# Windowed attention and a softplus layer on one core: later w_in transfers behind a maximum, the table of picks in five pieces, a new written-out sequence

## The chip, the cores and the metric

The kernel runs on one core of a Trainium2 chip. The metric is the device time of one execution in microseconds (us). Five engines work side by side: TensorE (PE in the profile, with PEld for its weight loads), VectorE (DVE), ScalarE (ACT), GpSimd (POOL) and SyncE (SP), which here only issues loads. POOL also issues loads (those that cast from 32 to 16 bit) and stores.

## The reference, cut to what matters

```python
# q, k, v: (8, 8, 576, 64) float32; global_idx: 8 positions; w_in (512, 2048), w_out (2048, 512)
scores = q @ k.T / 8
mask = (abs(pos[:, None] - pos[None, :]) <= 32) | is_global[:, None] | is_global[None, :]
attn = softmax(where(mask, scores, -1e9))
x = (attn @ v).transpose(0, 2, 1, 3).reshape(4608, 512)     # heads side by side
h = x @ w_in
out = (max(h, 0) + log1p(exp(-abs(h)))) @ w_out             # softplus between two products
```

## The kernel before, in words

**Tiling.** Each of the 8 batches has 18 blocks of 32 queries. Four blocks in a row (128 tokens, all 8 heads) are a *pair* of score tiles, one for each half of the heads: 36 pairs in all. Four pairs (512 tokens) are a *stage*, 9 stages. For a pair, PE makes scores `s` (`add_pair`), DVE takes the maximum `m`, ACT the exponential into `st` with its sum `sm`, DVE the reciprocal `rs`, POOL or DVE the product `pn` (`no` in the code), and DVE transposes `pn` into `pt` (`tp` in the code). In the first stage the mask is added on PE, by a matmul `s<-mask,ident`, and each half of the heads has its own maximum (`m`, 128x4).

**From attention to the layer.** `add_values` multiplies `pt` with `v` (kept as `vb`) into `xo`, and copies that to `xT`. The first stage is done in three pieces, of one, two and one pairs, the later ones mostly whole. The global columns enter through `vg`, which a chain of its own makes (`add_global`): scores of the global queries `sg`, maximum `gm` and `gnb`, exponential `pg`, transpose `pgt`, product with v `ov`, reciprocal `grs`. `add_moe` multiplies `xT` with the four tiles of `w_in` (`win` 0 to 3, each landing as two transfers) into `h`, ACT makes `g` by softplus, and PE multiplies `g` with `w_out` (`wout` 0 to 3) into `o`.

**Loads.** The q and k of batch 0 come by six loads on SP (`add_parts`): for each of the two, tokens 0-255, tokens 256-511 and the last 64; I call them q0, q1, q2 and k0, k1, k2 (the last 64 tokens are two transfers of 64 KB, the others one of 512 KB). They are cast to `qb` and `kb`, transposed on PE (`tr`) and copied into `qx` and `kx`; `qg` takes the global queries from the matmuls `pick<-hot`, which run over all of q, and the same over all of k fill the global columns of `kx`, which every score tile reads. The v of batch 0 comes by 8 casting transfers on POOL, w_in by 8 more behind a copy that waits for q1 (`T["held"]`), and w_out by 4 behind a copy that waits for batch 1's k1. Batch 1's q and k are queued on SP behind a tiny read of `win` 2 (`trail<-win`), which waits for its landing, and batch 1's v behind a tiny read of `wout` 0.

**What sets the order.** Every piece of work is a job with a cost. A planner (`_Order.run`) follows a written-out sequence of jobs and engines, `ORDER`, so that each engine's queue has a fixed order. The planner's costs (`SWITCH`, `SLOW`, `FETCH`, `moves`, `late`, `hold`) only place idle-time work: where it reckons that PE would stand still before 34 us, `keep` puts matmuls without use (`warm`) that keep PE's clock up. It reckons with PE's instructions being fetched in blocks:

```python
BLOCK = 256
ASK = 130
NEED = 448
```

that is, the first 448 instructions (a matmul and its weight load are two) are there at the start, and each 256 later ones come by a fetch that is asked for a few hundred instructions ahead. From batch 2 on a table `pick`, made by `make_pick` on DVE, gathers the global rows.

Of the kernel before, what the change touches and what calls it, by code (L numbers as in the profile page):

```python
# [20 lines left out]
class _Order:  # L21
# [16 lines left out]
    SWITCH = 107  # L38
# [72 lines left out]
    BEGIN = 3300  # L111
    PACKETS = {1: 1024, 2: 256, 4: 576, 8: 1152}

    def settle(self, dma):
# [1363 lines left out]
```

## Time and profile before

| what | value |
|---|---|
| three runs, us | 332.49, 333.22, 333.39 (median 333.22) |
| the profiled execution, us | 331.16 |
| its span, us | 329.1 |
| PE busy, us | 319.9, of them `warm` 13.9 |
| DVE, ACT, POOL busy, us | 219.9, 233.8, 196.0 |
| transfers | 42.14 MB, 128 GB/s over the span |

The profiled execution is a single one; its span runs from the first to the last instruction, and its own time is 2.1 us longer. Rows of the timeline give the start, the duration, the engine, the line of the kernel, the operation with output and input, and in brackets how long the engine stood idle before and what ended that. A row of the windows gives, for a stretch of time, each engine's busy time and number of instructions, then PE's granted clock (1.00 is full), the busy share of the transfer engines and what they moved.

### The profile page before, as it was taken

The numbers are of one execution on the slowest core, as the hardware profiler recorded it, in microseconds if no ns is written. First come the engines' busy times: TensorE is split into PE (matmuls) and PEld (weight loads), VectorE is DVE, ScalarE is ACT, GpSimd is POOL, SyncE is SP. The second block draws the span as 40 slices with busy tenths as digits, with TensorE's granted clock in tenths as the row PEclk, the third lists the DMA queues.
The fourth block names the chain that finished last, engine by engine and source line by source line (L and its number), as shares of the span: only waits on it lengthen the run. The fifth ranks groups of instructions, "written<-read, shape, count | busy, mean of one in ns | idle before, by whom it ended". The sixth has DMA issues, their size and how long they took to land.

```text
span 329.1 us, 12101 instructions
## 1 busy us (share of the span) xinstructions
PE 319.9 (97%) x5290; PEld 171.3 (52%) x5290; DVE 219.9 (67%) x386; ACT 233.8 (71%) x459; POOL 196.0 (60%) x175
## 2 busy tenths in 40 slices
PE   8878999999999999999999999999999999999996
PEld 3536876565555444544555445445544454454444
DVE  7796689847997799884995975378776970431000
ACT  5698879676798896488558857995749647914622
POOL 7827828996678567969587496738282927230000
PEclk9997999999999999999999999999999999999999
DMA  7998999999889899999999960370010012001002
GB/s 193 187 205 195 198 189 155 157 166 244 136 152 146 152 226 173 180 228 189 178 179 167 155 162 4 127 145 3 4 66 0 36 66 85 13 32 66 34 32 97
DMA packets 168796, 42.14 MB, mean 128 GB/s; under 512 B 153256, under 2 KB 165800, under 8 KB 168744
## 3 DMA queue, kind: packets, MB, share of 16 engines
q1 hardware_dynamic: 155928, 27.15, 46.8%
q0 software_dynamic: 10944, 11.08, 16.9%
q10 hardware_dynamic: 1872, 3.15, 2.5%
q8 instruction: 41, 0.67, 0.9%
q14 instruction: 11, 0.09, 0.1%
HBM read 36.71 MB, written 9.44 MB: 140 GB/s over the span
## 4 chain that ended last, share of the span: by engine, by line
PE 90%; DVE 2%; SPq 2%; DMA 2%; issue 1%; ACT 1%
PE o L1305 39%; PE h L1294 37%; PE xo L1259 4%; PE s L1085 4%; DMA stage<-in_q_dram 2%; PE ov L1005 2%; SPq L522 1%; PE pick L894 1%; SPq L526 1%; PE sg L976 1%; PE warm L737 1%; DVE qx L728 1%; PE tr L865 1%; DVE m L1100 1%; PE pick L907 1%
## 5 line engine op out<-in xcount | busy, mean ns | idle before, releaser
L1305 PE MATMUL o<-wout,g 128*128 128x512 bf16 (+1 forms) x592 | 138.3, 374 | 0.0
L1294 PE MATMUL h<-xT,win 128*128 128x512 bf16 (+3 forms) x768 | 137.8, 328 | 0.1
L1300 ACT ACTIVATE g<-h 128x512 bf16<-128x512 f32 (+3 forms) x192 | 84.5, 503 | 30.0 <-PE h L1294 27.0
L1140 POOL TENSOR_TENSOR pn<-st,rs 128x1024 bf16<-128x1024 f32 (+1 forms) x38 | 66.7, 1766 | 55.7 <-DVE rs L1134 49.9
L1294 PEld LDWEIGHTS <-win 128*128 128x128 bf16 x768 | 67.5, 99 | 59.6 <-issue 0.8
L1305 PEld LDWEIGHTS <-g 128*128 128x128 bf16 x592 | 55.9, 98 | 60.7 <-ACT g L1300 1.0
L1108 POOL TENSOR_TENSOR st<-st,m 128x1024 f32<-128x1024 f32 x32 | 60.2, 1894 | 27.1 <-DVE m L1102 27.0
L1089 DVE TENSOR_TENSOR st<-s,mask 128x512 f32<-128x512 f32 x64 | 41.1, 677 | 18.6 <-PE s L1085 18.4
L1132 DVE TENSOR_REDUCE sm<-st 128x8 f32<-128x1024 f32 x32 | 38.5, 1203 | 14.8 <-ACT st L1125 14.6
L1102 DVE TENSOR_REDUCE m<-st 128x8 f32<-128x1024 f32 x32 | 37.9, 1209 | 0.3
L728 ACT COPY osb<-o 128x512 f32<-128x512 f32 (+1 forms) x30 | 17.2, 577 | 22.6 <-PE o L1305 20.2
L1125 ACT ACTIVATE st<-st 128x1024 f32<-128x1024 f32 x32 | 32.7, 1052 | 0.3
L1149 DVE STREAM_TRANSPOSE pt<-pn 128x512 int32<-128x512 int32 x36 | 24.5, 690 | 5.2 <-POOL pn L1140 5.1
L728 ACT CAST xT<-xo 128x512 bf16<-128x512 f32 (+3 forms) x28 | 11.7, 467 | 18.8 <-PE xo L1259 18.8
L728 DVE CAST xT<-xo 128x512 bf16<-128x512 f32 (+3 forms) x20 | 11.3, 601 | 17.5 <-PE xo L1259 17.4
L1300 ACT ACT_TABLE_LOAD x15 | 19.2, 1283 | 1.7 <-PE h L1294 1.5
L1125 ACT ACT_TABLE_LOAD x14 | 18.0, 1283 | 0.7 <-ACT osb L728 0.4
L725 POOL TENSOR_SCALAR qb<-stage 128x1152 bf16<-128x1152 f32 (+2 forms) x15 | 16.8, 1126 | 2.2 <-issue 1.1
L1085 PE MATMUL s<-kx,qx 64*32 64x128 bf16 x1152 | 14.5, 220 | 3.6 <-issue 2.8
L1085 PEld LDWEIGHTS <-qx 64*32 64x32 bf16 x1152 | 10.4, 90 | 12.2 <-issue 8.9
L728 POOL CAST vb<-stage 128x1152 bf16<-128x1152 f32 x12 | 13.7, 1146 | 3.3 <-DMA stage<-in_v_dram 3.3
L737 PE MATMUL warm<-vb 128*128 128x512 bf16 x46 | 13.9, 451 | 1.3 <-DVE vb L559 1.3
(127 smaller groups left out, 287.2 us busy)
## 6 DMA issues: line engine op xcount, KB each, us to landing
stage<-in_v_dram SPq DMA_DIRECT2D x56, 144.0 KB, 4.2
stage<-in_q_dram SPq DMA_DIRECT2D x48, 144.0 KB, 3.7
stage<-in_k_dram SPq DMA_DIRECT2D x48, 144.0 KB, 4.0
out_dram<-osb POOLq DMA_DIRECT2D x24, 256.0 KB, 3.2
out_dram<-osb ACTq DMA_DIRECT2D x11, 256.0 KB, 2.0
stage<-in_q_dram SPq DMA_DIRECT2D x4, 512.0 KB, 6.2
stage<-in_k_dram SPq DMA_DIRECT2D x4, 512.0 KB, 6.9
win<-in_moe_w_in_dram POOLq DMA_DIRECT2D x8, 256.0 KB, 7.7
```

The source lines that it names most:

```text
L728: {"ACT": nc.scalar.copy, "DVE": V.tensor_copy, "POOL": nc.gpsimd.tensor_copy}[e](out, in_)
L1085: nc.tensor.matmul(out=PS["s", n, g][quad(a), x, :], lhsT=qx[b % 2][rows(g), a, j * BL:(j + 1) * BL], rhs=kx[b % 2][rows(g), a, e0 * BL:(e ...
L1089: V.tensor_tensor(out=PS["st", n][:, h, :, :], in0=PS["s", n, h][:, :, :], in1=mask[:, h, j0:j0 + PB, :, :].rearrange("p j s i -> p j (s i ...
L1102: V.reduce_max(out=m[:], in_=flat(PS["st", n], h0, h1), axis=AX)
L1108: on(e).tensor_tensor(out=t, in0=t, in1=over(PS["m", n, y][:], SL * BL), op=OP.subtract)
L1125: nc.scalar.activation(out=t, in_=t, func=AF.Exp)
L1132: V.reduce_sum(out=sm[:], in_=flat(PS["st", n], h0, h1), axis=AX)
L1140: on(e).tensor_tensor(out=PS["pn", n][:, :, :, h0:h1].rearrange("p x s h -> p h x s"), in0=PS["st", n][:, h0:h1], in1=PS["rs", n, y][:].re ...
L1149: V.transpose(out=bass.AP(base.tensor, base.offset, ap=[list(base.ap[0]), [2 * STEP, PB // 2], [STEP + BL // 2, 2], [1, SL * BL]]), in_=PS ...
L1294: nc.tensor.matmul(out=h[:, :], lhsT=w_in_t[c // 4][:, kd, c % 4 * P:(c % 4 + 1) * P], rhs=PS["xT", m][:, kd, lo:hi], start=(kd == 0), sto ...
L1300: nc.scalar.activation(out=PS["g", m, c][:, lo:hi], in_=PS[key][:, lo_of(c, hi - lo)], func=AF.Softplus)
L1305: nc.tensor.matmul(out=PS["o", m, ns, a][:, :], lhsT=PS["g", m, kf][:, ns * P:(ns + 1) * P], rhs=w_out_t[kf // 4][:, kf % 4, a:z], start=( ...
```

## The change

Three things are done. First, the second transfer of `win` 1 and all that follow it on POOL get a dependence on a new small copy on POOL, `T["seen"]`, which reads the maximum of pair 1 (its second half of the heads). Second, `make_pick` is cut: the clearing and three small steps stay together, and each of the four comparisons is a job of its own. Third, costs of the planner are changed and `ORDER` is replaced by another sequence.

```diff
-    SWITCH = 107
+    SWITCH = 96
...
-    FETCH = 4000
-    SLOW = ((27000, 8000), (34500, 6200), (55000, 8200), (230000, 6000), (1e9, 4500))
+    FETCH = 5500
+    SLOW = ((27000, 6000), (36500, 6800), (60000, 7000), (118000, 5500), (152000, 6300), (230000, 5500), (1e9, 5000))
+    CAP = 7500
...
-                took_ = max(next(x for until, x in self.SLOW if ask < until), self.backlog(ask + 1200) - ask + 2400)
+                took_ = max(next(x for until, x in self.SLOW if ask < until), min(self.backlog(ask + 3000) - ask, self.CAP) + 2400)
...
-    BEGIN = 3300
+    BEGIN = 2900
...
-    FILL, FILLT, NARROW, NFILL, NFILLT = 0.75, 220, 0, 0.8, 140
+    FILL, FILLT, NARROW, NFILL, NFILLT = 0.75, 220, 0, 0.93, 57
...
-    ORDER = (52, 57, 62, 162, 167, 122, 137, 146, 156, 4, 117, 113, 151, 141, 132, 127, 182, 172, 177, 187, 370, 9, 14, 213,
...
+    def make_picks(r):
+        V.tensor_tensor(out=pick[quad(r)].rearrange("p c e g -> p (c e) g")[:, :, r * NG:(r + 1) * NG],
+                        in0=posK[quad(r)].rearrange("p c e -> p (c e)").unsqueeze(2).to_broadcast([BL, 2 * NC, NG]),
+                        in1=gf[quad(r)].unsqueeze(1).to_broadcast([BL, 2 * NC, NG]), op=OP.is_equal)
+
     def make_pick():
...
-        for r in range(R):
...
+    LATER = (1, 1)
...
-            last = T["w_in", x] = o.add({"POOL": (650, 0)}, lambda e, x=x, y=y: weights_in(x, y), [last or T["held"]],
-                                        rank=-1 if x else 0, hold=2000 if x else 0, moves=1340)
+            last = T["w_in", x] = T["w_in", x, y] = o.add({"POOL": (650, 0)}, lambda e, x=x, y=y: weights_in(x, y), [last or T["held"]],
+                                        rank=-1 if x else 0, moves=1340)
+            if (x, y) == LATER:
+                T["later"] = last
...
+        if not m:
+            T["seen"] = o.add(pool(190), lambda e: nc.gpsimd.tensor_copy(seen[:, 0, :], PS["m", 1, 1][:, 0:1]), [T["mx", 1, 1]], rank=0, uses=[("m", 1, 1)])
+            T["later"]["deps"].append(T["seen"])
```

What the new sequence does to the queues shows at three places. On SP, the first loads of batch 0 stood like this before (`stage_60` receives q, `stage_61` k):

```order
L531 DMA gi<-in_global_idx_dram 128x16
L522 DMA stage_60<-in_q_dram 128x8x128
L522 DMA stage_61<-in_k_dram 128x8x128 x2
L522 DMA stage_60<-in_q_dram 128x8x128
L526 DMA stage_61<-in_k_dram 64x4x64 x2
L526 DMA stage_60<-in_q_dram 64x4x64 x2
L765 DMA trail<-win_126 1x2x1
```

and in the changed kernel like this:

```order
L534 DMA gi<-in_global_idx_dram 128x16
L525 DMA stage_61<-in_k_dram 128x8x128 x2
L529 DMA stage_61<-in_k_dram 64x4x64 x2
L525 DMA stage_60<-in_q_dram 128x8x128
L529 DMA stage_60<-in_q_dram 64x4x64 x2
L525 DMA stage_60<-in_q_dram 128x8x128
L769 DMA trail<-win_126 1x2x1
```

All of k now comes first, and q1, which stood fourth, is last.

On POOL, from v's transfers to the first products `pn`, before (`seen` is the small copies' target, `mask<-mask` is `make_ends`):

```order
L725 TENSOR_SCALAR qb_64<-stage0_60 128x2x4x64
L477 DMA vb0_66<-in_v_dram 32x18x64 x8
L1373 COPY seen_110<-stage0_60 128x1
L1356 DMA win0_124<-in_moe_w_in_dram 64x4x512 x2
L671 COPY mask_78<-mask_78 128x2x256
L1356 DMA win1_125<-in_moe_w_in_dram 64x4x512 x2
L1356 DMA win2_126<-in_moe_w_in_dram 64x4x512 x2
L1356 DMA win3_127<-in_moe_w_in_dram 64x4x512 x2
L1140 TENSOR_TENSOR pn_735<-st_415,rs_680 128x512
L1140 TENSOR_TENSOR pn_763<-st_488,rs_731 128x512
```

and now (`pn_533` is pair 0's; pair 0's two stood on DVE before):

```order
L480 DMA vb0_66<-in_v_dram 32x18x64 x2
L1379 COPY seen_110<-stage0_60 128x1
L1360 DMA win0_124<-in_moe_w_in_dram 64x4x512
L675 COPY mask_78<-mask_78 128x2x256
L1360 DMA win0_124<-in_moe_w_in_dram 64x4x512
L1438 COPY seen_110<-m_444 128x1
L1360 DMA win1_125<-in_moe_w_in_dram 64x4x512 x2
L1360 DMA win2_126<-in_moe_w_in_dram 64x4x512 x2
L1144 TENSOR_TENSOR pn_533<-st_316,rs_522 128x512
L1144 TENSOR_TENSOR pn_533<-st_316,rs_511 128x512
L1360 DMA win3_127<-in_moe_w_in_dram 64x4x512
L1144 TENSOR_TENSOR pn_670<-st_404,rs_661 128x512
```

In POOL's queue the new copy stands ahead of the third transfer already, so that six of the eight wait for it, and pair 0's products follow four of them.

On DVE, around the first maxima, before:

```order
L728 COPY kx_70<-tr 128x4x4x32 x2
L723 TENSOR_SCALAR qb<-stage_60 128x256
L1100 TENSOR_REDUCE m<-s 128x4 x2
L728 CAST qg_72<-pick 64x4x8 x2
L728 COPY qx_68<-tr 128x4x128
L1100 TENSOR_REDUCE m<-s 128x4
L982 TENSOR_REDUCE gm<-sg 128x1 x2
L983 TENSOR_REDUCE gnb<-gm 128x1
```

and now:

```order
L727 TENSOR_SCALAR qb<-stage_60 128x256
L647 TENSOR_SCALAR mask<-eqF 128x2x9x8 x2
L732 COPY kx_70<-tr 128x4x4x32
L679 TENSOR_TENSOR own<-posM,gf 128x9x2x8
L727 TENSOR_SCALAR qb<-stage_60 128x2x4x64
L1104 TENSOR_REDUCE m<-s 128x4 x2
L732 COPY qx_68<-tr 128x4x128
L732 CAST qg_72<-pick 64x4x8 x2
L1104 TENSOR_REDUCE m<-s 128x4
L732 COPY qx_68<-tr 128x4x128
L986 TENSOR_REDUCE gm<-sg 128x1 x2
L987 TENSOR_REDUCE gnb<-gm 128x1
```

A cast of one half of q1 (`128x2x4x64`) now stands right ahead of pair 0's maxima; before, it was the cast of q2 (`128x256`).

More of the change, by code (lines that the diff above doesn't have):

```diff
@@ L142, in settle @@
                 sent.append(self.PACKETS[job["units"]])
-            self.backs.append((t, now))
+            if q:
+                self.backs.append((t, now))
             done[q] += 1
@@ L154 @@
     WARM = 0
-    FILL, FILLT, NARROW, NFILL, NFILLT = 0.75, 220, 0, 0.8, 140
-    COLD, COLDT, LONG = 5400, 427, 0.93
+    FILL, FILLT, NARROW, NFILL, NFILLT = 0.75, 220, 0, 0.93, 57
+    COLD, COLDT = 5400, 427
     STARVE = 900
@@ L172, in keep @@
         if t0 < self.COLD:
-            span = (t1 - t0) * self.LONG
+            span = (t1 - t0) * 0.93
             cold = min(span, self.COLD - t0)
@@ L287, in run @@
                 mine = "POOL" if "POOL" in j["cost"] else "SP"
-                dma.append((mine, t + 1500 if j["cost"][e][0] else t, j["moves"], j))
+                dma.append((mine, t + (1900 if mine == "POOL" else 1500) if j["cost"][e][0] else t, j["moves"], j))
                 j["at"] = t
@@ L599, in make_pick @@
                         scalar1=pi[:, 1:2], scalar2=None, op0=OP.add)
-        for r in range(R):
-            V.tensor_tensor(out=pick[quad(r)].rearrange("p c e g -> p (c e) g")[:, :, r * NG:(r + 1) * NG],
-                            in0=posK[quad(r)].rearrange("p c e -> p (c e)").unsqueeze(2).to_broadcast([BL, 2 * NC, NG]),
-                            in1=gf[quad(r)].unsqueeze(1).to_broadcast([BL, 2 * NC, NG]), op=OP.is_equal)
     def make_band():
@@ L759, with follow @@
     followed = set()
-    def follow(x, t):
+    def follow(x, t, row):
         if x in followed:
@@ L764, in follow @@
         followed.add(x)
-        nc.sync.dma_start(out=trail[x:x + 1, :], in_=t[D:D + 1, t.shape[1] - 1, t.shape[2] - 2:])
+        nc.sync.dma_start(out=trail[x:x + 1, :], in_=t[row:row + 1, t.shape[1] - 1, t.shape[2] - 2:])
     def add_load(b, w, deps):
@@ L775, in add_load @@
                     last = T["half", 0, h] = o.add({"POOL": (1300, 0)}, lambda e, h=h, x=x: load_v(nc.gpsimd, 0, h, range(2 * x, 2 * x + 2)), [last], rank=0,
-                                                   moves=1200, late=200)
+                                                   moves=1080, late=200)
                     T["cast", 0, 2].append(last)
@@ L782, in emit @@
                     if behind:
-                        follow(1, w_out_t[0])
+                        follow(1, w_out_t[0], D)
                     load_v(nc.sync, b, h, range(R))
@@ L795, in emit @@
                 if b:
-                    follow(0, w_in_t[2])
+                    follow(0, w_in_t[2], D)
                 load_part(b, w, t)
             T["part", b, w, t] = o.add({"DMA": (700 if b else 0, 0)}, emit, had(("w_in", 2)) + T["cast", 0, w] if b else [], rank=0,
-                                       moves=(1800 if b else 1900) if t < FULL else 900 if b else 650, units=1 if t < FULL else 2)
+                                       moves=1800 if t < FULL else 900 if b else 650, units=1 if t < FULL else 2, late=0 if t < FULL or b else 700)
     def add_cast(b, w):
@@ L947, in add_prep @@
             ws = (1, 0)
-            job = o.add({"PE": (560, 730)}, lambda e, ws=ws: pck(e, ws), [x for w in ws for x in T["cast", b, w]] + [T["make_pick"]],
+            job = o.add({"PE": (560, 730)}, lambda e, ws=ws: pck(e, ws), [x for w in ws for x in T["cast", b, w]] + T["make_picks"],
                         rank=4, array=32, ins=72, opens=[("pick", key)])
@@ L1042, in add_global @@
             ovs.append(o.add({"PE": (72 * n, 72 * n + 170) if b else (110 * n + 100, 110 * n + 240)}, lambda e, m0=m0, m1=m1: ov(e, m0, m1), [tps[-1], *ovs, *T["cast", b, 2]],
-                             rank=3, array=32, ins=16 * n, opens=[] if ovs else [("ov", ("ov", b, y)) for y in range(two)], uses=[("ov", b, y) for y in range(two)] if ovs else []))
+                             rank=3, array=34, ins=16 * n, opens=[] if ovs else [("ov", ("ov", b, y)) for y in range(two)], uses=[("ov", b, y) for y in range(two)] if ovs else []))
         T["gexp", b], T["tpg", b], T["ov", b] = exps[-1], tps[-1], ovs[-1]
@@ L1275, in add_values @@
             last = o.add({"PE": (t, t + 170)}, lambda e, s0=s0, s1=s1: val(e, s0, s1), ready if last is None else [last] + (had(("gv", 0)) if ahead else []),
-                         rank=1, array=64, urgent=last is None, ins=16 * (s1 - s0) + (8 if ahead and s0 == 0 else 0), opens=opened if last is None else [],
+                         rank=1, array=65, urgent=last is None, ins=16 * (s1 - s0) + (8 if ahead and s0 == 0 else 0), opens=opened if last is None else [],
                          uses=[("pt", m)] + ([("xo", v_, r) for r in range(KD)] if last is not None else []))
@@ L1392 @@
     setup("make_own", lambda e: make_own(e), {"DVE": (230, 310)}, [T["make_first"], T["part", 0, 0, 1]], rank=2, port=True)
-    setup("make_pick", lambda e: make_pick(), {"DVE": (1800, 1890)}, [T["make_own"], T["load", 0, 2]], rank=9, hold=18000)
+    setup("make_pick", lambda e: make_pick(), {"DVE": (620, 700)}, [T["make_own"], T["load", 0, 2]], rank=9, hold=18000, port=True)
+    T["make_picks"] = [setup(("make_picks", r), lambda e, r=r: make_picks(r), {"DVE": (310, 390)}, [T["make_pick"]], rank=9, port=True) for r in range(R)]
     setup("blank", lambda e: blank(nc.gpsimd, 1), pool(900), [T["load", 0, 2]], rank=6, hold=11000)
@@ L1439 @@
                 T["w_out", a] = o.add({"POOL": (800, 0)}, lambda e, a=a: weights_out(a),
-                                      [T["landed"], T.get(("w_out", a - 1))], rank=-1, hold=800 if a else 0, moves=2700)
+                                      [T["landed"], T.get(("w_out", a - 1))], rank=-1, moves=2700, late=1500)
         for x in range(len(VALS)):
```

1 line of the change is left out of this document (added), and 143 rows, old and new, of the table ORDER.

## Prediction

> **What bounds the kernel now.** I read the page first: who is busy, and which chain ended last.
>
> ```profile
> PE 319.9 (97%) x5290; PEld 171.3 (52%) x5290; DVE 219.9 (67%) x386; ACT 233.8 (71%) x459; POOL 196.0 (60%) x175
> PE 90%; DVE 2%; SPq 2%; DMA 2%; issue 1%; ACT 1%
> ```
>
> PE is busy for 319.9 of 329.1 us, so 9.2 us are idle, and 90% of the chain is PE. The useful matmuls are the same in both kernels; only what PE loses can change. So I looked for the losses in PE's timeline.
>
> ```profile
> 22.89 0.41 PE L1085 MATMUL s<-kx,qx 64*32 64x128 bf16 x30
> 26.14 0.23 PE L1085 MATMUL s<-kx,qx 64*32 64x128 bf16 x2 [2.84 <-issue]
> 26.30 0.48 PE L1245 MATMUL xo<-vb 128*128 128x128 bf16 x4
> 27.08 0.37 PE L1259 MATMUL xo<-pt,vg 32*64 32x128 bf16 x8
> 28.20 4.33 PE L1294 MATMUL h<-xT,win 128*128 128x128 bf16 x60
> 32.36 0.81 PE L737 MATMUL warm<-vb 128*128 128x512 bf16 x3
> 33.25 0.93 PE L1259 MATMUL xo<-pt,vb 32*64 32x32 bf16 x80
> 34.34 0.39 PE L865 MATMUL tr<-ident,kb 128*128 128x128 bf16 x4
> 45.65 0.38 PE L1305 MATMUL o<-wout,g 128*128 128x512 bf16 x1
> ```
>
> The first layer matmul starts at 28.20. Just before, PE stops after 30 of the 32 matmuls of a score tile and waits 2.84 us for no other engine ("issue"). By the order of the program the two that are late begin at instruction 704, which is 448 + 256: a boundary of the blocks that the code itself names. I read the gap as a late instruction fetch. After 34.34 I found no gap on PE above 0.4 us up to the last matmul, so the game is decided before 45 us. The granted clock shows a second price of the gap:
>
> ```profile
> 25.00:26.00 1.00, 0.00 (x0) 0.00 (x0) 0.50 (x4) 1.00 (x8) 0.48 (x1) 1.00 1.09 182
> 29.00:30.00 1.00, 1.00 (x13) 1.00 (x11) 0.45 (x2) 1.00 (x8) 0.56 (x1) 0.55 1.15 338
> 30.00:31.00 1.00, 1.00 (x22) 1.00 (x20) 0.97 (x3) 0.98 (x7) 0.53 (x1) 1.00 1.19 303
> ```
>
> The clock is 0.55 near 29.5 and full a microsecond later; PE begins 13 matmuls in the one and 22 in the other. At 22 in a microsecond the 60 first `h` need 2.7 us, not 4.33, so the cold clock took 1.6. The Trainium skill (TensorE: Matmul & The Clock Gate, Part 1) has the clock halved after an idle window of about 3.4 us; here 2.84 us of idle were enough, so the row decides, and short gaps may cost clock as well.
>
> **The change, part by part.** First the loads, since q1 is now last of six: two half-microsecond windows, then the page's transfers, and the timelines of POOL and DVE.
>
> ```profile
> 9.00:9.50 0.50, 0.50 (x4) 0.26 (x3) 0.43 (x3) 0.32 (x1) 0.50 (x2) 1.00 1.20 293
> 10.50:11.00 0.50, 0.50 (x10) 0.38 (x9) 0.00 (x0) 0.00 (x0) 0.50 (x1) 1.00 1.82 172
> 6.17 5.59 POOL L477 DMA_DIRECT2D vb<-in_v_dram  x8
> vb<-in_v_dram POOLq DMA_DIRECT2D x8, 72.0 KB, 6.3
> win<-in_moe_w_in_dram POOLq DMA_DIRECT2D x8, 256.0 KB, 7.7
> 15.07 0.39 DVE L723 TENSOR_SCALAR qb<-stage 128x256 bf16<-128x256 f32 x1 [0.22 <-DMA stage<-in_q_dram]
> 15.41 1.29 DVE L1100 TENSOR_REDUCE m<-s 128x4 f32<-128x512 f32 x2
> ```
>
> SP's loads run alone at 293 GB/s until v's transfers, issued from 6.17, join them near 9.5; the rate falls to 172. The last load, q2, lands at 15.07. Up to 9.5 some 1.8 MB have moved, which now is k0, k1, k2, q0 (1.70) and most of q2 (0.13); left are about 0.55 MB, nearly all q1. Before, 0.56 MB were left and took 5.5 us; by bytes q1 lands at 15.0. Counted in packets (512 bytes each by the tiles' rows, where half of what was left before had 256), there are two thirds as many: 3.6 us, 13.1. v starts at the same time within 0.5 us, since two small operations take the place of the cast ahead of it on POOL. I take 14.4, nearer to the bytes, as the queue is full either way.
>
> From there to pair 0's `pt` DVE runs in order, with the cast of half of q1 ahead of the maxima:
>
> ```profile
> 16.70 0.39 DVE L728 CAST qg<-pick 64x32 bf16<-64x32 f32 x2
> 17.12 0.73 DVE L728 COPY qx<-tr 128x512 bf16<-128x512 bf16 x1
> 24.60 0.71 DVE L1149 STREAM_TRANSPOSE pt<-pn 128x512 int32<-128x512 int32 x1
> 17.76 0.67 DVE L1100 TENSOR_REDUCE m<-s 128x4 f32<-128x512 f32 x1
> 22.96 0.72 DVE L1140 TENSOR_TENSOR pn<-st,rs 128x512 bf16<-128x512 f32 x1
> 20.76 1.23 PE L1005 MATMUL ov<-vb,pgt 32*32 32x129 bf16 x72 [0.29 <-DVE pgt L995]
> 25.52 4.04 POOL L1140 TENSOR_TENSOR pn<-st,rs 128x512 bf16<-128x512 f32 x4 [7.11 <-DVE rs L1134]
> 14.73 3.68 POOL L1356 DMA_DIRECT2D win<-in_moe_w_in_dram  x6
> 27.45 0.29 DVE L728 CAST xT<-xo 128x128 bf16<-128x128 f32 x1 [0.36 <-PE xo L1259]
> ```
>
> Before, this took 25.31 - 15.07 = 10.2 us. Now two products (1.45) leave DVE; the longer cast adds 0.3, a late copy of the last q columns 0.4, and `grs`, put ahead of `pt`, waits for `ov` (1.23, less a maximum of 0.67 beside it, and the way there: 0.9). That makes 10.2 - 1.45 + 1.6 = 10.35; the plain sum of the rows on the way is 10.75, since rows overlap a little. I take 10.75, as steps wait for PE here and there, and `pt` is there at 25.2, as before. POOL keeps pace: the maximum that `seen` reads is DVE's fourth step, 14.4 + 0.65 + 1.29 + 0.73 + 0.39 + 0.67 = 18.1; four issues at 0.61 and two products at 1.01 end at 22.9. So the hold costs w_in's third transfer 3.6 us (14.73 to 18.3).
>
> PE then takes `xo` at 25.2 instead of 26.30, if its instructions are there. They are asked for near 17.5 in both kernels; the old request fell on all eight transfers of w_in, the new one on the first two. `vg` comes at 25.6, `xo` ends at 26.0, and with 0.75 to the copy's end (27.45 to 28.20 before) `h` starts at 26.7: 1.5 earlier, warm.
>
> Next late are pairs 1 and 2. The last two products on POOL need two more maxima on DVE (0.67 each, with a cast of 0.3 and small ones: 27.4), 2.0 us, and a transpose of 0.7: their `xo` starts at 30.2 instead of 33.1. PE has `h` until 26.7 + 48/22 = 28.9 and three `warm` until 29.6, so it waits 0.6. Then 1.0 of `xo`, 0.75 for 16 `h`, four `warm` at 0.25 (32.36 to 33.10 for three): 32.95. ACT says about the same:
>
> ```profile
> 16.14 0.37 ACT L1121 ACTIVATE st<-s,m 128x128 f32<-128x128 f32 x1
> 16.49 0.36 ACT L1121 ACTIVATE st<-s,m 128x128 f32<-128x128 f32 x1
> 30.93 1.28 ACT L1300 ACT_TABLE_LOAD   x1
> 32.23 1.64 ACT L1300 ACTIVATE g<-h 128x128 bf16<-128x128 f32 x9
> ```
>
> its last 8 exponentials (0.35 each) follow `xT` at 26.7, then the table 1.28 and eight `g` 1.46 make 32.2, and two copies of `xT` about 33.0. From that point the same PE work is left as from 34.34 before. Gain: 1.35 us.
>
> What the hold takes back lies with batch 1.
>
> ```profile
> 25.30 0.73 SPq L765 DMA_DIRECT2D trail<-win  x1
> 26.14 1.02 SPq L522 DMA_DIRECT2D stage<-in_k_dram  x2
> 31.52 1.61 DVE L728 CAST kb<-stage 128x512 bf16<-128x512 f32 x2 [0.39 <-DMA stage<-in_k_dram]
> 35.89 0.84 POOL L1360 DMA_DIRECT2D wout<-in_moe_w_out_dram  x1
> 43.74 0.65 SPq L765 DMA_DIRECT2D trail<-wout  x1
> 40.06 1.56 DVE L601 TENSOR_TENSOR pick<-posK,gf 32x144 bf16<-32x144 f32 x4
> 77.22 0.69 PE pick L894 x34
> ```
>
> Queued behind `seen` on POOL are the rest of w_in, `pn` and w_out; behind the read of `win` 2 on SP, batch 1. `win` 2 lands at about 26.2 (issue near 20.5, and the 7.7 us of the page less the shorter queue) against 25.30: batch 1 is 0.9 us later while PE is 1.35 earlier. Its first transposes now stand behind 16 wider `h` (1.7 us), which hides that. w_out's first transfer, 35.89 before, comes at 36.9, and lands 7.85 us later (43.74 - 35.89 before) at 44.75; PE reaches its first `o` at 45.65 - 1.35 = 44.3. That is a wait of 0.45 with ends 0 (POOL reaches it at the old time) and 1.4 (batch 1 comes 2 us late). I take 0.25, since a small wait ahead of it would move PE too.
>
> The table of picks: five pieces, the same work (the four comparisons are 1.56 us on DVE before 42 us), first needed by batch 2 near 77 us; cost nothing, and two of them move behind the copies that batch 1's scores wait for. Fewer `warm` (42 for 46) are inside the gaps above. Elsewhere PE has work without gaps: nothing.
>
> Sum: -1.35 + 0.25 = -1.1 us. The profiled execution has 331.16 us (span 329.1) and would have 330.1; it ran 2.06 us under the median, from which I count: 333.22 - 1.1 = 332.1.
>
> **The rivals.** *The loads come early.* If the packet count is right, q1 lands at 13.1 and all of the chain moves by 1.3: -2.4, 330.8. For it: 512-byte packets ran at 293 GB/s; against: v's transfers share the engines until 17.
>
> *The fetch stays late.* It took from about 17.3 to 26.14, 8.8 us. Asked at 17.6 it would arrive at 26.4, with the clock gone again; or the next block, asked for in the middle of the held transfers, stops the second `xo`. Then about 333.2. Only two transfers lie ahead of the first request, which speaks against. The Trainium skill (Runtime: NRT & Kernel Launch, Instruction fetch mechanics) says that instructions come in blocks of 256, which agrees with the place of the gap, and that the fetch is mostly hidden; by that the gap would have another cause and stay, also 333.2. The trace has it in plain sight, so I give that little.
>
> *q1 last makes it slower.* Its half stands ahead of every maximum on DVE, so each microsecond of it is one of the whole head. If the engines serve v first, it lands with v's last transfer, issued at about 11.1 and landing 6.3 later, at 17.4: 3.0 later than I take, -1.1 + 3.0 = +1.9, 335.1. It decides from 15.5 (no change); at 16.5 the kernel is 1 us slower. For it: the last 0.26 MB before took 4 us.
>
> **How the numbers follow.** A difference of 0.3%, 1.0 us, is about what a measurement can tell. The forecast (332.1, its own range 331.0 to 332.9) has 0.50, of which 0.29 are faster by more than that and 0.21 not. Early loads 0.14, faster. The late fetch 0.16: 0.03 faster, 0.12 same, 0.01 slower. q1 too late 0.20: 0.02 same, 0.18 slower. Together 0.46 faster, 0.35 same, 0.19 slower. The range reaches from 330.2, below the early case, to 334.2, half-way into the late one.
>
> **What would show it.** The cast of `qb` (128x512) on DVE near 14.4; `seen` near 18.2; no "issue" gap of over 1 us on PE before `xo`, and the clock at 1.00 from 26 to 31; first `h` near 26.7, first wide `h` (128x256) near 33.0; the first `o` near 44.5. I am wrong if q1 lands after 15.5, if a gap of the old size stands at another block boundary, or if `o` waits over 1 us for `wout`.

## The result, and the profile after

The changed kernel takes 337.33 us (median of 4 runs, 336.16 to 339.69) against 333.31 for the kernel before: the ratio is 1.0154, 95% interval 1.011 to 1.0198. It is slower by 4.0 us, where 1.1 us faster was forecast, and above the forecast's range. Ratios and intervals go by fast executions alone and medians by all, so a ratio need not be the quotient of the two medians (1.0121 here). The profiled execution has 338.14 us, its span 336.4.

Single executions differ more than the three times of before let one think. The kernel before ran again beside every group of experiments below: its times lie between 330.7 and 337.4, nearly half of them near 331.3 and most others near 333.2. A likely reason comes out below (late blocks of instructions). So each ratio is to be read with its interval, and 1 us between two kernels says little.

First the page's lines of after (busy times, and the shares of the chain that ended last):

```profile
PE 321.5 (96%) x5286; PEld 169.3 (50%) x5286; DVE 220.3 (65%) x386; ACT 229.5 (68%) x453; POOL 201.8 (60%) x182
PE 80%; DMA 10%; SPq 5%; ACT 2%; issue 1%; POOL 1%; DVE 0%; ACTq 0%
```

PE is idle for 14.9 us, not 9.2, and 10% of the chain is now DMA where it was 2%. PE's timeline says where (start, duration, the idle time before in brackets):

```profile
24.50 0.40 PE L1249 MATMUL xo<-vb 128*128 128x128 bf16 x4
26.20 1.95 PE L1298 MATMUL h<-xT,win 128*128 128x128 bf16 x32
29.09 1.05 PE L1298 MATMUL h<-xT,win 128*128 128x128 bf16 x16 [0.94 <-DMA win<-in_moe_w_in_dram]
33.72 1.91 PE L1298 MATMUL h<-xT,win 128*128 128x256 bf16 x16
36.54 0.40 PE L869 MATMUL tr<-ident,kb 128*128 128x128 bf16 x4 [0.91 <-DVE kb L732]
42.03 0.40 PE L869 MATMUL tr<-ident,qb 128*128 128x128 bf16 x4 [0.59 <-POOL qb L729]
47.22 0.59 PE L1309 MATMUL o<-wout,g 128*128 128x512 bf16 x2
62.48 0.80 PE L1009 MATMUL ov<-vb,pgt 32*32 32x129 bf16 x72 [1.71 <-DVE m L1106]
66.49 2.12 PE L1309 MATMUL o<-wout,g 128*128 128x512 bf16 x9 [0.52 <-ACT g L1304]
...
175.14 0.53 PE L1263 MATMUL xo<-pt,vb 32*64 32x96 bf16 x43 [2.19 <-issue]
```

The head went as forecast: no gap for a late fetch before `xo`, which starts at 24.50; the first `h` stands at 26.20 (28.20 before, 26.7 forecast). But the lead melts: `h` waits 0.94 for `win`, the first wide `h` is at 33.72 (forecast 33.0), batch 1's transposes wait 0.91 and 0.59, and the first `o` comes at 47.22, 1.6 later than before. Then come two losses in places where I had forecast none: 1.71 and 0.52 us at 62 to 66 us, and 2.19 us without a releaser at 173 us.

Why is `ov` late? The next rows are SP's queue, then POOL's and ACT's of after, each a timeline:

```profile
28.98 0.73 SPq L769 DMA_DIRECT2D trail<-win  x1
29.81 1.00 SPq L525 DMA_DIRECT2D stage<-in_k_dram  x2
45.49 0.64 SPq L769 DMA_DIRECT2D trail<-wout  x1
46.17 9.53 SPq L480 DMA_DIRECT2D stage<-in_v_dram  x8
```

```profile
15.35 0.44 POOL L1379 COPY seen<-stage 128x1 f32<-128x1 f32 x1 [2.23 <-DMA stage<-in_q_dram]
18.85 0.19 POOL L1438 COPY seen<-m 128x1 f32<-128x1 f32 x1 [1.30 <-DVE m L1104]
19.08 2.45 POOL L1360 DMA_DIRECT2D win<-in_moe_w_in_dram  x4
34.48 0.44 POOL L1449 COPY seen<-stage 128x1 f32<-128x1 f32 x1 [2.54 <-DMA stage<-in_k_dram]
39.37 0.62 POOL L729 TENSOR_SCALAR qb<-stage 128x512 bf16<-128x512 f32 x1 [2.42 <-PE xo L1263]
39.94 0.85 POOL L1364 DMA_DIRECT2D wout<-in_moe_w_out_dram  x1
```

```profile
61.23 1.15 ACT L732 CAST vb<-stage 128x1152 bf16<-128x1152 f32 x1 [2.40 <-DMA stage<-in_v_dram]
62.29 2.00 ACT L1129 ACTIVATE st<-st 128x1024 f32<-128x1024 f32 x2
66.16 0.28 ACT L1304 ACTIVATE g<-h 128x128 bf16<-128x128 f32 x1
```

Each link is late: `win` 2 has landed at 28.98 (25.30 before), so batch 1's k is issued at 29.81 (26.14); `wout` 0 follows at 39.94 (35.89), the read of it comes at 45.49 (43.74), and batch 1's v, queued behind that read, is issued from 46.17 for 9.53 us (44.44, 7.62). Its second half is cast at 61.23, after ACT has stood idle for 2.40 us for it, and only then can `ov` run (62.48) and, further down ACT's queue, the `g` of 66.16 for which `o` waits 0.52. The profile puts the idle time of `ov` down to a maximum on DVE that also ended just then; the row of ACT has the cause. In all five executions of the new order in which `ov` waits, it starts 0.10 us after the end of this cast, whatever the profile names. In the kernel before the same cast, on POOL, came 5 us earlier, and `ov` did not wait:

```profile
44.44 7.62 SPq L477 DMA_DIRECT2D stage<-in_v_dram  x8
...
55.99 1.14 POOL L728 CAST vb<-stage 128x1152 bf16<-128x1152 f32 x1
...
58.15 0.80 PE L1005 MATMUL ov<-vb,pgt 32*32 32x129 bf16 x72
```

One link is the new order's own. The copy that gates `wout`, which reads k1, stands at 34.48, earlier than before (35.37). What keeps `wout` 0 is the cast of `qb` at 39.37: the new order puts this cast of batch 1's q0 ahead of it on POOL, and q0, issued at 30.98, lands 8.2 us later. (The row names `xo`; with v freed, in an experiment below, the profile puts the same wait down to the landing of q.) No run moves `wout` 0 alone.

### The profile page after: what moved, and what is told of

Its sections match the earlier page's. It is cut to its first block, busy times and chain, and to the rows that moved or that the text cites. A ratio compares the mean times of both kernels' runs of the same rounds, so it can differ in the third digit from the quotient of the medians.

```text
span 336.4 us, 12089 instructions
## 1 busy us (share of the span) xinstructions
PE 321.5 (96%) x5286; PEld 169.3 (50%) x5286; DVE 220.3 (65%) x386; ACT 229.5 (68%) x453; POOL 201.8 (60%) x182
## 4 chain that ended last, share of the span: by engine, by line
PE 80%; DMA 10%; SPq 5%; ACT 2%; issue 1%; POOL 1%; DVE 0%; ACTq 0%
PE o L1309 34%; PE h L1298 33%; PE xo L1263 4%; PE s L1089 3%; SPq L480 3%; DMA win<-in_moe_w_in_dram 2%; DMA stage<-in_q_dram 2%; DMA stage<-in_v_dram 2%; DMA stage<-in_k_dram 2%; DMA wout<-in_moe_w_out_dram 2%; PE ov L1009 1%; SPq L529 1%; PE pick L898 1%; SPq L525 1%; PE sg L980 1%
## 5 line engine op out<-in xcount | busy, mean ns | idle before, releaser
L1304 ACT ACTIVATE g<-h 128x512 bf16<-128x512 f32 (+3 forms) x192 | 83.5, 500 | 36.8 <-PE h L1298 35.5
L1298 PEld LDWEIGHTS <-win 128*128 128x128 bf16 x768 | 66.5, 98 | 59.5 <-issue 1.5
L1144 POOL TENSOR_TENSOR pn<-st,rs 128x1024 bf16<-128x1024 f32 (+1 forms) x39 | 67.9, 1750 | 32.5 <-DVE rs L1138 24.5
L1093 DVE TENSOR_TENSOR st<-s,mask 128x512 f32<-128x512 f32 x64 | 41.4, 680 | 18.2 <-PE s L1089 18.0
L732 ACT COPY osb<-o 128x512 f32<-128x512 f32 (+1 forms) x28 | 16.0, 572 | 19.2 <-PE o L1309 18.3
L732 ACT CAST xT<-xo 128x512 bf16<-128x512 f32 (+3 forms) x25 | 10.8, 484 | 16.7 <-PE xo L1263 16.7
L1321 POOL DMA_DIRECT2D out_dram<-osb x24 | 13.9, 580 | 10.8 <-DVE osb L732 9.3
L729 POOL TENSOR_SCALAR qb<-stage 128x1152 bf16<-128x1152 f32 (+2 forms) x15 | 17.8, 1204 | 2.6 <-PE xo L1263 2.4
L1263 PE MATMUL xo<-pt,vb 32*64 32x96 bf16 (+2 forms) x1328 | 14.4, 210 | 2.4 <-issue 2.4
L732 POOL CAST kb<-stage 128x1152 bf16<-128x1152 f32 (+1 forms) x9 | 11.9, 1328 | 6.2 <-PE h L1298 5.6
L1263 PEld LDWEIGHTS <-vb 32*64 32x64 bf16 x1328 | 13.7, 102 | 3.3 <-issue 2.6
```

The costliest lines, as they stand in the source:

```text
L732: {"ACT": nc.scalar.copy, "DVE": V.tensor_copy, "POOL": nc.gpsimd.tensor_copy}[e](out, in_)
L1093: V.tensor_tensor(out=PS["st", n][:, h, :, :], in0=PS["s", n, h][:, :, :], in1=mask[:, h, j0:j0 + PB, :, :].rearrange("p j s i -> p j (s i ...
L1144: on(e).tensor_tensor(out=PS["pn", n][:, :, :, h0:h1].rearrange("p x s h -> p h x s"), in0=PS["st", n][:, h0:h1], in1=PS["rs", n, y][:].re ...
L1263: nc.tensor.matmul(out=PS["xo", v_, c][h * D:(h + 1) * D, (x - X0) * BL:(z - X0) * BL], lhsT=lhs, rhs=rhs, start=start and not ahead, stop ...
L1298: nc.tensor.matmul(out=h[:, :], lhsT=w_in_t[c // 4][:, kd, c % 4 * P:(c % 4 + 1) * P], rhs=PS["xT", m][:, kd, lo:hi], start=(kd == 0), sto ...
L1304: nc.scalar.activation(out=PS["g", m, c][:, lo:hi], in_=PS[key][:, lo_of(c, hi - lo)], func=AF.Softplus)
```

## The experiments

Theory A: the hold makes w_in, and with it batch 1 and v, late. Theory B: the new sequence costs whatever the transfers do. Theory C: the hold does keep the first late fetch away, and lifting it brings it back. Theory D came with the first results: w_in is late since its old gate, the small copy that reads q1, waits for what is now the last load. Every ratio is to the kernel before on the same chip.

| kernel | median us (lowest) | ratio, 95% interval |
|---|---|---|
| after, no hold | 335.44 (333.44) | 1.0070, 1.0030 to 1.0111 |
| before, hold alone | 333.04 (332.47) | 1.0020, 0.9985 to 1.0054 |
| after, batch 1 behind win 0 | 336.77 (334.85) | 1.0112, 1.0027 to 1.0196 |
| after, v freed | 334.35 (332.61) | 1.0056, 1.0018 to 1.0095 |
| after, gate q0, no hold | 336.84 (333.51) | 1.0105, 1.0058 to 1.0151 |
| after, no hold, v freed | 335.33 (332.80) | 1.0072, 1.0042 to 1.0102 |
| after, gate q0, no hold, v freed | 332.73 (331.61) | 1.0020, 0.9983 to 1.0058 |
| after, gate q0, hold, v freed | 334.65 (332.75) | 1.0062, 1.0027 to 1.0097 |
| after, v freed, batch 1 behind win 1 | 334.52 (333.13) | 1.0067, 1.0028 to 1.0107 |
| before, v freed | 332.30 (331.21) | 0.9993, 0.9950 to 1.0037 |
| after, table in one piece | 336.15 (334.77) | 1.0113, 1.0080 to 1.0147 |
| before, 16 fewer warm | 336.50 (334.27) | 1.0112, 1.0045 to 1.0179 |
| before, rows moved by 8 | 332.84 (331.32) | 0.9996, 0.9956 to 1.0037 |
| after, rows moved by 8 | 337.56 (335.49) | 1.0137, 1.0068 to 1.0206 |
| after, rows moved by 8, v freed | 335.62 (334.06) | 1.0131, 1.0036 to 1.0225 |

### The hold lifted

```diff
-nc.gpsimd.tensor_copy(seen[:, 0, :], PS["m", 1, 1][:, 0:1])
+nc.gpsimd.tensor_copy(seen[:, 0, :], natural(0, 1)[:, 0, 0, 0, 0:1])
```

> The changed kernel, with the small copy reading the staged q1 instead of the maximum, so that w_in's third and later transfers are no longer held; all queues keep their order. Theory A (the hold costs): win 2 lands near 25.5 instead of 28.9, batch 1's k is issued near 26.3 instead of 29.8, the waits of PE at 29 (0.94), 36.5 (0.91), 42 (0.59), 62 (1.71) and 66 us (0.52) go, the time is 334.0 or less. Theory B (the new sequence costs, whenever the weights come): the wait at 62 us stays above 1 us and the time is 336.5 to 338. Theory C (the hold keeps the early fetch in time): an idle time of PE with no releaser of 2 us or more comes back before the first h, and takes up to 3 us of what A gives.

It gains (1.0070 instead of 1.0154), but not in the way of theory A. Timeline rows of this run, of POOL, SP and PE:

```profile
15.07 0.44 POOL L1379 COPY seen<-stage 128x1 f32<-128x1 f32 x1 [1.92 <-DMA stage<-in_q_dram]
17.37 2.47 POOL L1360 DMA_DIRECT2D win<-in_moe_w_in_dram  x4
...
28.16 0.72 SPq L769 DMA_DIRECT2D trail<-win  x1
...
25.97 0.47 PE L1263 MATMUL xo<-pt,vb 32*64 32x64 bf16 x38 [1.51 <-issue]
32.16 0.68 PE L1263 MATMUL xo<-pt,vb 32*64 32x96 bf16 x61 [1.19 <-issue]
62.65 0.80 PE L1009 MATMUL ov<-vb,pgt 32*32 32x129 bf16 x72 [1.53 <-POOL pn L1144]
```

`win` 2 lands only 0.8 earlier (28.16), not 3.4, since the other gate still waits for q1 until 15.07. The wait at 62 us stays at 1.53. Theory C has the direction, not the size: a late fetch of 1.51 us stands before the first `h` and one of 1.19 before the second `xo`. Over all profiles of the new order the gap at that first boundary is 0 to 1.03 us in nine executions with the hold, and 1.04 to 1.51 in four without.

### The hold alone, in the kernel before

```diff
 V.reduce_max(out=m[:], in_=PS["s", n, h0][:], axis=AX, negate=True)
+if (n, y) == (1, 1):
+    nc.gpsimd.tensor_copy(seen[:, 0, :], m[:, 0:1])
+    for x_, y_ in HELD:
+        weights_in(x_, y_)
```

> The kernel before with the hold alone: w_in's third and later transfers wait for the same maximum, all else in the old sequence. Theory A: win 2 lands near 28.5 instead of 25.3, batch 1 and w_out come 3 us later, the time is 335.5 to 337. Theory B: 332.3 to 334.3. Theory C: the 2.84 us before the first h go, which gives back up to 2 us of A's loss.

(`HELD` are both halves of `win` 1 to 3.) No change that can be measured: `win` 2 lands at 27.63, PE waits 1.26 for `kb` and 0.80 for `qx`, and yet the time is the same; the late fetch stays (2.53 of 2.84). In this order `wout` 0 stands ahead of the cast of q0 on POOL: it is issued at 37.45, its read comes at 43.08 (43.74 without the hold), and `ov` does not wait. So theory A is wrong as put: the late `win` 2 costs in the new order, not in the old. Of theory C's gain the old order sees little.

### Batch 1 earlier, v freed

```diff
-follow(0, w_in_t[2], D)
+follow(0, w_in_t[0], D)
```

> The changed kernel, with batch 1's q and k queued behind the landing of win 0 instead of win 2; the hold stays. Theory A, with the chain of landings as the link: batch 1's k is issued before 26 us, the waits at 36.5, 42 and 62 us go, 334.0 to 335. Its rival: the loads of batch 1 now share the transfer engines with win 1 to 3, h waits longer at 29 us (over 2 us instead of 0.94), and the time is 337 or more. Theory B: the wait at 62 us stays, 336.5 to 338.

The rival came true in its waits (its 337 was just missed): k is issued at 22.56, but `h` waits 4.3 us in three places for `win`.

```diff
-if behind:
+if False:
     follow(1, w_out_t[0], D)
```

> The changed kernel without the read of wout 0 ahead of batch 1's v, so that v is queued right behind batch 1's q and k. If the landing of v is what PE waits for at 62 us: that wait (1.71) and the 0.52 at 66 us go, 335.0. If it is the casts on ACT, whatever the landing: the wait stays and the time is 337. Rival: v's transfers delay w_out, the first o starts a microsecond or more after 47.2, and the time is 337 or more.

This gives back 3.0 us, the most of any single edit. v is issued from 36.69, its cast on ACT starts at 57.88 without a wait, and both waits at 62 and 66 us are gone. The first `o` waits 0.37 for `wout`. So the chain through v is shown as a cause. The control, the same edit in the kernel before:

> The kernel before without the read of wout 0 ahead of batch 1's v. If freeing v only repairs what the change broke (in the old sequence PE never waited for v at 58 us): within 1 us of the kernel before, 332 to 334. If it is a gain in any sequence: 331 or less. If v's transfers now delay w_out, which PE reached at 45.65 without a wait: the first o waits, 334 or more.

Nothing (0.9993): v's read of `wout` 0 was harmless until the change made `wout` and all behind it late.

### Both gates, and all three

```diff
-nc.gpsimd.tensor_copy(seen[:, 1, :], natural(0, 1)[:, 0, 0, 0, 0:1])
+nc.gpsimd.tensor_copy(seen[:, 1, :], natural(0, 0)[:, 0, 0, 0, 0:1])
```

> The changed kernel with both small copies on POOL reading the staged q0, which lands near 10.4 us, instead of q1 (15.3) and the maximum (18.9): w_in has neither gate, as far as POOL's queue allows (v's issues end at 13.1). Theory D (w_in is late since its old gate waits for q1, and q1 is now loaded last): win 0 is issued at 13.1 and win 2 lands at 26 or earlier, where the run without the hold alone had 28.2; batch 1's k is issued 2 us or more earlier than there (28.98). Theory A (only the hold): as without the hold, win 2 within 0.7 us of 28.2. For the time: 333 to 335 if an earlier batch 1 helps; its rival is that w_in now shares the transfer engines with q1, which lands at 16.3 or later instead of 15.1 and pushes the first h later by as much: 336 or more. By theory C the idle time with no releaser ahead of 27 us is 1.5 us or longer.

(The other small copy reads q0 as well here, which lifts the hold.) Theory D's landing is shown: `win` 2 lands at 26.32 instead of 28.16. The first `o` is 1.45 earlier than without the hold alone (45.80, 47.25). The time does not follow (336.84): v is still issued only from 45.12, `ov` waits 0.87, and the ten times fall in two groups, 333.5 to 334.6 and 336.5 to 339.3.

The next three are the edits shown so far, put together.

> The changed kernel without the hold and without the read of wout 0 ahead of batch 1's v, the two edits together. If the two losses lie apart: 335.4 less the 2.1 to 3.0 us that freeing v gave alone, 332.4 to 333.3, the waits at 62 and 66 us gone, and the late fetches of the run without the hold (1.5, 1.2 and 0.7 us) still there. If lifting the hold only helped by bringing v earlier: no better than freeing v alone, 334.0 to 335.

Neither sum was met in its number: 335.33, no better than without the hold alone or with v freed alone, though the profiled execution (332.80) has no wait at 62 us. I could not show what the slower executions of this kernel lose.

> The changed kernel with w_in gated by q0 alone, without the hold and with batch 1's v freed: of its changes the new order of the work stays, and q1 last. If the loss of the changed kernel is late transfers (w_in behind q1, then batch 1, then v): win 2 lands near 26.3, no wait of PE above 0.5 us for kb, w_out or v between 30 and 70 us, and the time is 333.3 or less but for late instructions. If something else of the new order costs too: those waits are gone and the time is 334 or more without idle time that has no releaser; if late instructions are what is left, that idle time is there and makes up the difference to 333.

With gate, hold and v all lifted, the changed kernel equals the one before (332.73, ratio 1.0020, interval across 1). Timeline rows of it, of POOL, SP and PE:

```profile
13.03 0.20 POOL L1379 COPY seen<-stage 128x1 f32<-128x1 f32 x1
13.17 0.64 POOL L1360 DMA_DIRECT2D win<-in_moe_w_in_dram  x1
...
25.48 0.73 SPq L769 DMA_DIRECT2D trail<-win  x1
36.50 15.96 SPq L480 DMA_DIRECT2D stage<-in_v_dram  x8
...
25.59 0.47 PE L1263 MATMUL xo<-pt,vb 32*64 32x64 bf16 x38 [1.04 <-issue]
31.82 0.68 PE L1263 MATMUL xo<-pt,vb 32*64 32x96 bf16 x61 [1.24 <-issue]
46.23 0.61 PE L1309 MATMUL o<-wout,g 128*128 128x512 bf16 x2 [0.70 <-DMA wout<-in_moe_w_out_dram]
```

`win` is issued from 13.17, `win` 2 lands at 25.48 as in the kernel before (25.30). After 50 us PE has no gap. What it still loses is two late fetches (1.04, 1.24) and 0.70 for `wout`. So the new order by itself, q1 last included, costs nothing that can be measured; the late transfers do. q1 did not even need the gate: with w_in sharing the engines from 13.2 on, it was cast on DVE at 15.12, against 15.32 in the changed kernel.

> The changed kernel with w_in gated by q0 and batch 1's v freed, but with the hold: against the run with all three lifted (332.73, ratio 1.002) only the hold is put back. If the hold costs by itself, as the chain of late transfers has it: win 2 lands near 28 again instead of 25.5, waits of PE for win at 29 us and for kb at 36 us come back, 1 us or more slower, 333.8 or more. If what the hold keeps in time (the blocks of instructions, late by 1.04 and 1.24 us in that run) pays for it: those idle times are under 0.5 us each and the time is 332.2 to 333.3.

With the hold alone put back: 1.0062. The first case of the expectation by its time and by the landing (`win` 2 at 28.00, 25.48 without the hold), not by its waits: the late fetches stay (1.02, 0.41), and the first `o` now waits 1.68 for `wout`. The intervals of the two runs overlap, so that the hold costs by itself is likely and not shown.

```diff
-follow(0, w_in_t[2], D)
+follow(0, w_in_t[1], D)
...
-if behind:
+if False:
     follow(1, w_out_t[0], D)
```

> The changed kernel with v freed as before and batch 1's q and k queued behind win 1 instead of win 2. If what is left of the loss (334.35 against 332.9) is batch 1 coming late (waits of 0.9 for kb at 36 us, 0.4 for w_out at 46 us): k is issued near 26.5 instead of 28.9, both waits go, 333.0 to 333.6. Rival: as with win 0, its transfers delay win 2 and win 3, h waits for win by a microsecond or more before 36 us, 334.5 or more.

The read ahead of k comes at 26.19 instead of 28.08, and the time stays (1.0067 against 1.0056): `o` waits 0.85 for `wout`, `h` 0.62 for `win`: a mild form of the rival.

### The table

```diff
-setup("make_pick", lambda e: make_pick(), ...)
+setup("make_pick", lambda e: (make_pick(), *[make_picks(r) for r in range(R)]), ...)
...
-setup(("make_picks", r), lambda e, r=r: make_picks(r), ...)
+setup(("make_picks", r), lambda e: None, ...)
```

> The changed kernel with the table of picks made in one piece again (the four comparisons follow the clearing at once, on DVE). If cutting it costs or gains nothing, as forecast: the same as the changed kernel, 336 to 339. If the pieces were what kept DVE free for batch 1's copies: 1.2 us of comparisons in a row delay a copy into kx or qx between 36 and 46 us, PE waits there by up to 1 us more, 338 or more. If instead the later pieces hurt where they stand now, 336 or less.

336.15, at the lower end of what "no effect" would give; its interval overlaps that of the changed kernel. Nothing is shown either way beyond about 1 us.

### Late blocks of instructions

> The kernel before, once more, for a second profile: its 25 times lie in two groups, near 331.3 and near 333.2. If this one is of the upper group, an idle time of PE of about 2 us that the first profile (331.16) lacks, with no releaser and at a boundary of 256 instructions, would show that the groups are late fetches; a lower clock or longer matmuls would show something else. If it is of the lower group: no such idle time besides the 2.84 us before the first h.

> The changed kernel, once more, for a second profile. The waits at 62 (1.71) and 66 us (0.52) and the three between 29 and 43 us come again, as the order sets them. The idle time of 2.19 us at 173 us has no releaser: if it is chance it is gone or elsewhere, if it belongs to the new sequence it is there again within 0.5 us.

The kernel before, in this execution 335.48 us, has in PE's timeline:

```profile
26.14 0.29 PE L1085 MATMUL s<-kx,qx 64*32 64x128 bf16 x2 [2.66 <-issue]
39.48 1.59 PE L1294 MATMUL h<-xT,win 128*128 128x256 bf16 x13 [1.12 <-issue]
45.95 0.21 PE L868 MATMUL tr<-ident,qb 64*64 64x64 bf16 x1 [0.77 <-issue]
52.42 1.04 PE L1305 MATMUL o<-wout,g 128*128 128x512 bf16 x4 [0.99 <-issue]
```

Beside the known one there are three late fetches of together 2.88 us that the first profile lacks. The half clock after the known one also lasts twice as long, 6.8 us (25.73 to 32.55) for 3.4, which by an estimate at twice the pace is 1.7 us more. Together that is about the 4.3 us between the two profiled executions. That the groups near 331.3 and 333.2 differ in the same way is likely and not shown. The changed kernel's second profile (337.80) has no gap at 173 us, but two others:

```profile
25.39 0.47 PE L1263 MATMUL xo<-pt,vb 32*64 32x64 bf16 x38 [0.46 <-issue]
31.68 0.68 PE L1263 MATMUL xo<-pt,vb 32*64 32x96 bf16 x61 [0.75 <-issue]
63.63 0.98 PE L1009 MATMUL ov<-vb,pgt 32*32 32x129 bf16 x72 [2.54 <-DVE pt L1153]
```

The wait of `ov` came again, and larger. So the wait belongs to the order, the gap at 173 us to the execution: it came in one other run, at the same 43 matmuls before the end of that `xo` (1.94 us, the run with batch 1 behind win 1). What lies there is seen in the transfers of one microsecond (packets, MB, share of the 16 engines):

```profile
q1 hardware_dynamic: 784, 0.20, 130.0%
q8 instruction: 1, 0.02, 8.2%
```

The packet of instructions travels at the end of a jam of 784 packets of batch loads, and PE goes on 2.8 us after it starts. The row is within 10 of a boundary 448 + 256 x 23. The 19 profiles have 37 such gaps of 0.3 us or more. Each lies within 10 rows of a boundary 448 + 256 n, 16 of them at row 704, and PE goes on 2.2 to 3.0 us after the start of the packet (found by narrowing the stretch of this view). At none of the 760 boundaries does PE go on sooner than that. A test of that reading, in the kernel before:

```diff
+if n > 20 and not started:
+    started.append(1)
+    nc.gpsimd.memset(idle[:], 0)
+    n -= 16
```

> The kernel before with 16 of its first 29 warm matmuls left out and the other 13 started about 2.5 us later (behind a clearing of their operand on POOL), so that PE's instructions move by 32 and the boundary at row 704 falls into the second product xo instead of two matmuls before its first. If the idle time of 2.84 us is a late block of instructions: it shrinks to 0.3 to 1.5 us and stands inside xo, the first h starts at 27.0 to 27.8 instead of 28.2 and with less cold clock, the time is 331 to 332. If it belongs to that place in the work (the last two matmuls of a score tile wait for something unseen): it stays at 2.5 us or more in front of the same two matmuls, and the time is 333.

```profile
21.11 0.24 PE L1092 MATMUL s<-kx,qx 64*32 64x128 bf16 x6 [0.37 <-issue]
25.68 0.26 PE L1266 MATMUL xo<-pt,vb 32*64 32x64 bf16 x10 [0.32 <-DVE rs L1141]
27.14 0.32 PE L1266 MATMUL xo<-pt,vb 32*64 32x96 bf16 x26 [1.20 <-issue]
```

Only the first group of `warm` (29 matmuls) meets the condition. With 32 instructions fewer ahead, the gap moved into `xo`: PE stops at exactly row 704, now in the 64x96 part, and a smaller gap of 0.37 stands at row 448. The gap hangs on the count, not on the work. But the time is worse (336.50): other boundaries now have gaps, of 0.97 at 45 us, 1.12 at 140 us and 2.06 at 272 us. The last does not need busy transfers: the transfer engines' share is 0.39 in the microsecond in which its packet starts (269.67) and 0 in the next two, but PE has gone through the 256 rows ahead of it in 1.1 us.

```diff
-for x in range(n):
+for x in range(n - (4 if n > 20 else 0)):
```

> The changed kernel with 4 of its first 21 warm matmuls left out, which end at 8.4 us, at most 1 us of idle time more: all later instructions of PE have numbers 8 lower. If late blocks of instructions hang on where the boundaries fall in the work: the idle time without a releaser is redistributed, at places 8 rows later in the work (the one at 173 us, if it comes, with 39 instead of 43 matmuls of that xo left), and the time may move by up to 2 us either way from 337.3. If it is chance between executions alone: the spread of the times is as large as before and the median within 1 us of 337.3.

> The kernel before with 4 of its first 29 warm matmuls left out: the boundary at row 704 falls 8 rows later in the work, after the last two matmuls of the score tile and the first two of xo. The idle time of 2.8 us before those two goes to the middle of xo and shrinks to about 1 (26.1 against 25.2 to 25.5, when pt and the exponentials are there), the first h comes at 27.5 to 28.0 and the time is 331.5 to 332.3, if the later blocks come in time as before. If the other boundaries matter as much: new idle times without a releaser between 35 and 55 us or in the loads of later batches, and 333.5 or more.

> The changed kernel with v freed and the boundaries moved by 8 rows. With v freed alone 334.35. If the boundaries matter little: 333.8 to 334.9. If they matter: the median moves by more than 1 us, and the idle time without a releaser in its profile, against the 0.35 us of the run with v freed alone, says by how much.

```profile
27.16 0.29 PE L1247 MATMUL xo<-vb 128*128 128x128 bf16 x2 [2.86 <-DVE m L1102]
```

In the kernel before the gap moved by just these 8 rows, behind the first two `xo` (the maximum that the row names is not what they wait for: in the kernel before the same `xo` ran at 26.30, ahead of that maximum). It did not shrink as expected, since the packet came later too (24.6, 23.8 before). Neither kernel changed (0.9996, 1.0137): with the boundaries moved by these 8 rows the changed one's loss stays. With v freed as well the wait at 62 us is gone, but the time of four runs (1.0131, interval to 1.0225) shows no gain; why is open.

## Why the prediction was wrong, point by point

The step that failed is "what the hold takes back": 0.25 us was put for late transfers that cost more than the whole gain. It rests on a landing of `win` 2 that came 2.8 us later than put, and it stops too early in the queue.

- *q1 lands at 14.4.* Its cast started at 15.32, near the bound by bytes (15.0) and above it. It is mis-sized by 0.9 us, and paid for elsewhere: the first `h` came earlier than forecast. (v's transfers were issued from 5.33, 0.84 earlier than before, where 0.5 was the bound.)
- *`seen` near 18.2, first `h` at 26.7, no late fetch before `xo`.* Right in the result: 18.85, 26.20, none in this execution (0.46 in the next). The executions without the hold have the longer gaps (1.04 to 1.51, with it 0 to 1.03), so the hold seems to help. But my reading of the fetch was wrong: I took the packet of 17.3 for the late one; PE waits for the next, at 23.8, and goes on 2.3 us later. In after that packet starts at 22.78, 1.05 us earlier, and row 704 has moved into the products of `pt` in the first `xo`, which start at 24.83; PE goes on there at 25.04, 2.3 us after the packet's start. That so little was left of the gap is in part luck.
- *First wide `h` at 33.0, a gain of 1.35.* It is 33.72, a gain of 0.62. Against the forecast stands the wait of 0.94 for `win` at 29 us, which the sum did not have.
- *"win 2 lands at about 26.2".* This step failed first. The issue near 20.5 was right; its landing took 8.07 us on the chain of after (from 20.89), where 5.7 was put, and 28.98 came of it. I took 2.0 off the page's median of 7.7 for a shorter queue, though this very transfer had needed 8.74 before (16.54 to 25.28). I also laid all of the delay on the hold. There are two causes, and they overlap. With the hold and the old gate the read of `win` 2 comes at 28.08 to 29.14 (six executions), with the hold alone at 28.00, with the gate alone at 27.44 and 28.16, with neither at 25.48 and 26.32. So either alone costs about 2 us, and lifting one gives little. The gate is w_in's old one: it reads q1, which the change had made the last load. I had described that gate and did not move it with its load.
- *"What the hold takes back": 0.25, with ends 0 and 1.4.* The term that decides. I followed the chain to `wout` and the first `o` and stopped there: 45.65 became 47.22, where 44.5 was forecast. `wout` was issued 3.0 us later than I put (39.94 for 36.9) and landed faster (5.53 for 7.85), so that the first `o`, late by the waits ahead of it, did not wait for it, and the sign of error that I had named (`o` waits over 1 us) did not show. The chain goes on: v stands on SP behind `wout` 0, and PE lost 2.2 us at 62 to 66 us for it (2.5 in the second profile). Freeing v gave 3.0 us.
- *"Elsewhere PE has work without gaps: nothing."* Wrong for that reason, and for a second: the fetch gap at 173 us, which is chance from one execution to the next. That the profiled execution of before ran 2 us under its median was a sign of it; I counted from the median and did not ask why.
- *Table in five pieces: 0.* Not contradicted, and not measured better than 1 us.
- *Rivals.* "q1 last makes it slower" had the sign, and its price of 335.1 was the nearest, but its mechanism (DVE's maxima behind a late q1, from 15.5 on) did not come; q1 hurt through POOL's gate. "The next block stops the second `xo`" is seen (0.20 here, 0.75 in the next execution, 1.19 without the hold), not as a return to 333.2. By the Trainium skill (Runtime: NRT & Kernel Launch, Instruction fetch mechanics) instructions come in blocks of 256 and the cost of crossing a boundary is mostly hidden. The first agrees with the moved gap at row 704. The second holds for most boundaries here, 37 of 760 having a gap of 0.3 us or more, but not at row 704, where 16 of 19 executions have one, of up to 2.86 us.

## What to carry to other kernels

When a load changes its place in a queue, look for every gate that reads its data, and move the gate or price the new wait. Follow a delayed transfer through all that is queued behind its landing until a link has slack that a row shows, not until the first engine that could absorb it. And before comparing kernels by 1 us, profile the old one twice: if its times fall in groups, late instruction blocks may be the larger effect.

## What the runs showed of the hardware

- PE can stand still for a block of its instructions, here for 0.3 to 2.9 us, at rows near 448 + 256 n. Most of these gaps came while batch loads kept the transfer engines full (a share of 130% in the row above), one (2.06 us) with the engines nearly idle, after PE had gone through 256 rows in 1.1 us. Which boundaries have a gap changes from one execution of the same program to the next; with the half clock that went with them this was 4.3 us between two executions of the kernel before (331.16, 335.48).
- The clock's answer to short gaps of PE differs from run to run. In the changed kernel gaps of 1.05 and 1.11 us, at 12 to 16 us, were followed by half the clock from 17 on:

```profile
17.00:18.00 1.00, 1.00 (x38) 0.41 (x40) 0.84 (x3) 1.00 (x7) 0.54 (x2) 0.50 0.67 65
18.00:19.00 1.00, 1.00 (x16) 0.26 (x11) 0.91 (x2) 1.00 (x7) 0.15 (x1) 0.50 1.14 181
```

(the third number from the end is the clock). Without the hold, gaps of 0.87 and 1.20 us in the same place left it at 1.00. The Trainium skill (TensorE: Matmul & The Clock Gate, Part 1) says that activity is judged in windows of about 3.4 us that run freely. The profiles agree: half the clock lasted 3.41 us (16.53 to 19.94 in after, 26.48 to 29.89 in before) or twice that. On the grid of 3.41 us that the clock's changes give in each of the 19 profiles, every window at full clock with 1.76 us or more of idle PE was followed by half the clock, and none with 1.35 or less was. In after the window from 13.12 to 16.53 held 1.40. So short gaps add up where they fall into one window; between 1.4 and 1.7 us both came, and what decides there is open.
